# The last output tile computed as two column halves in PSUM tiles of their own, with a new order list

## The chip, the cores and the metric

The kernel runs on one core of a Trainium2 chip. The metric is the device time of one execution in microseconds (us), the median of several runs. TensorE is called PE below and its weight loads PEld, VectorE is DVE, ScalarE is ACT, GpSimd is POOL, SyncE is SP.

## The reference

An attention over pooled keys and values is followed by a gated feed-forward block, in float32:

```python
B, H, S, D = q.shape                       # 8, 8, 576, 64
k_p = k.reshape(B, H, S // 8, 8, D).mean(axis=3)     # 72 pooled keys
v_p = v.reshape(B, H, S // 8, 8, D).mean(axis=3)
attn = softmax(q @ k_p^T / sqrt(D))
x = (attn @ v_p) as (B, S, 512)
h = relu(x @ w_in)                         # w_in 512 x 1024
conv = sum over 3 taps of conv_w[k] * (h shifted along S)
out = (h * sigmoid(conv)) @ w_out          # w_out 1024 x 512
```

## The kernel before

The batch of 8 is worked through in order. The attention of a batch element makes pooled and transposed keys (`attn_k`), transposed queries (`attn_q`), scores with the exponential on ACT (`attn_s`), and the weighted values, normalised on DVE (`attn_av`, line 687 writes `xx`). `mm1` (line 747) computes the hidden layer in 8 blocks of 128 features, with relu on ACT (line 753). `conv` makes the gate in one of two ways: on ACT and DVE (`conv_off`), or by diagonal matrices on PE (`conv_pe`, line 800, its gate on ACT at line 805); line 838 multiplies gate and hidden layer into `gT`.

`mm2` (line 860) is the output product. Two batch elements make a pair of 1152 rows, which are 9 tiles of 128 rows and 512 columns. Each tile sums over 8 contraction blocks: 8 matmuls of 512 columns into one PSUM tile `psfB` or `psfA`, a copy to SBUF (`oe`, line 883) and a store from SP (line 887). In the last pair the tiles 4 to 8 are cut: blocks 0 to 5 first, blocks 6 and 7 when the last gate product has come. The last tile of all, tile 8, has `final` set. Its blocks 0 to 5 are six matmuls of 512 columns; blocks 6 and 7 are done twice, for the columns 0 to 255 and then 256 to 511, as four matmuls of 256 columns. All ten write the same PSUM tile. Two copies of 256 columns (line 873) on ACT and two stores (line 878) from SP follow, one for each half.

PSUM has eight slots: three pairs of banks, A0 to A2, and two single banks, B0 and B1. Nothing picks a slot at run time. `PARAMS["order"]` is a list, written out by a planner, of all 1075 operations in the order in which they are given to their engines. An entry `562@A1` says operation 562 with its output in slot A1; an entry `25A0/82@B1` says that 25 units of 128 columns of filler matmuls on zeros (`fill`, line 231; four units make one matmul of 512 columns) go to PE into slot A0 ahead of operation 82. An operation that takes a slot waits until the reader of that slot's former content is done. `PARAMS["act"]` says which of the copies and elementwise operations run on ACT; the others run on DVE.

The operations named later, by their numbers in the list:

- 77 `kT.0` and 79 `kz.0.1` (line 507): the first transposed keys and the second of their copies on ACT.
- 82, 80, 84 `qT.0...` (line 567): the first batch element's query transposes in three groups, 24, 24 and 48 small matmuls on PE, each with a copy on ACT (line 573). The first two need the first part of the load of `q` (line 250, 64 rows), the third needs the second part.
- 110 `sc.0.4.0` (line 627) and 111: the first scores on PE and their exponential on ACT (line 633).
- 266 `mm2.0.0.0`: the first output tile of the first pair.
- 562 `av.4.2` and 564 `nm.4.2`: weighted values of batch element 4 and their normalisation on DVE (line 687). 604 `mm1.3.5`, 464 `convs.2.1` (line 800) and 465, its gate on ACT (line 805).
- 661 and the DVE and ACT copies after it: the load of `q` for batch element 6 from POOL (line 255) and its regrouping (line 261).
- 1058 and 1062: the copies of tiles 5 and 6 of the last pair. 1068 to 1074: the last tile, in the order of the diff below.

Of the kernel before, what the change touches and what calls it, by code (L numbers as in the profile page):

```python
# [13 lines left out]

PARAMS = {
    "order": (
# [40 lines left out]
    ),  # L57
    "act": (
# [84 lines left out]
def kernel(  # L143
# [10 lines left out]
    nc = tc.nc  # L154
# [3 lines left out]
    P = 128  # L158
    HC = S // 2
    n_dc = d_model // P  # L160
    n_fb = d_ff // P
# [53 lines left out]
    pl = Planner()  # L215
# [17 lines left out]
    def copy_on(e):  # L233
        return nc.scalar.copy if e == "ACT" else nc.vector.tensor_copy
# [609 lines left out]
    def mm2(pair, tiles, cuts=(0, n_fb), kind="o", final=False):  # L844
# [5 lines left out]
        for x, t in enumerate(tiles):  # L850
# [1 line left out]
            key = (kind, pair, t)  # L852
            ok = ("op", pair, t)
            for c0, c1 in zip(cuts, cuts[1:]):
                parts = [(0, 512)] if not final or c1 < n_fb else [(0, 256), (256, 512)]
                for y, (j0, j1) in enumerate(parts):
                    def fn(e, t=t, c0=c0, c1=c1, key=key, j0=j0, j1=j1):
                        a = slot(key)
                        for c in range(c0, c1):
                            nc.tensor.matmul(out=a[:, 0, j0:j1], lhsT=g[:, c, t * P:(t + 1) * P],  # L860
                                             rhs=w_out[:, c, j0:j1], start=(c == 0), stop=(c == n_fb - 1), skip_group_check=final)
                    i = pl.add(f"mm2.{pair}.{t}.{c0}" + (f".{y}" if len(parts) > 1 else ""), "PE", (0.2165 * (j1 - j0) / 512 + 0.002) * (c1 - c0), fn,
                               reads=[("gT", pair % 2, c, z) for c in range(c0, c1) for z in halves] + [("wo", 0), ("wo", 1)]
                               + ([ok] if c0 else []),
                               writes=[ok + (y,)] if len(parts) > 1 else [ok], take=key,
                               after=last_o[0] if not c0 else None)
                    if not c0:
                        last_o[0] = i
            if final:
                oi = None  # L870
                for y in range(2):
                    def fn(e, y=y, key=key):
                        copy_on(e)(out=osb[i3][:, 0, y * 256:(y + 1) * 256], in_=slot(key)[:, 0, y * 256:(y + 1) * 256])
                    oi = pl.add(f"oe.{pair}.{t}.{y}", {"ACT": 0.28, "DVE": 0.34}, 0, fn,
                                reads=[ok + (y,)], writes=[("osb", i3, y)], give=key if y else None, after=oi)

                    def fn(e, y=y):
                        nc.sync.dma_start(out=out_rows[r:r + P, y * 256:(y + 1) * 256], in_=osb[i3][:, 0, y * 256:(y + 1) * 256])
# [89 lines left out]
```

## Time and profile before

| what | value |
|---|---|
| time, median of 3 runs | 198.35 us (197.63, 198.35, 200.87) |
| the profiled execution | 196.67 us |
| its span, first to last instruction | 195.0 us |
| mean granted TensorE clock | 1.000 |
| HBM read, written | 32.52 MB, 9.44 MB |
| matmuls on PE, weight loads | 1730, 1746 |

A row of the timeline has the start, the duration, engine, line, operation, names of output and inputs, shape and count, and in square brackets the idle time before it and what ended it. Instructions of one kind that follow each other are one row. A row of the chain of waits has the start, the duration and the work that the end of the execution can be followed back to. Instructions of one engine overlap: the duration of one is longer than the distance to the next. In a group's row stand count, busy time, mean duration in ns, and idle time before the group. Of the 1746 matmuls 16 have no record in this trace, their weight loads have.

### The profile page before, as it was taken

How to read it: one execution, taken by the hardware profiler on the slowest of the kernel's cores; microseconds unless marked ns; L12 is line 12 of the kernel's file. 1: busy time of each engine (PE TensorE's matmuls, PEld its weight loads, DVE VectorE, ACT ScalarE, POOL GpSimd, SP SyncE). 2: the span in 40 equal slices, each digit the busy share in tenths (PEclk: the TensorE clock that was granted, in tenths of full speed). 3: DMA queues.
4: the chain of work that ended last, by engine and by line, in shares of the span. 5: the costliest groups of instructions: out<-in, count | busy, mean ns of one | idle time of the engine just before them, and what ended most of it. 6: DMA issues, size and time to landing. Idle time of an engine off the chain costs nothing.

```text
span 195.0 us, 4515 instructions
## 1 busy us (share of the span) xinstructions
PE 186.5 (96%) x1730; PEld 124.3 (64%) x1746; DVE 166.1 (85%) x388; ACT 167.0 (86%) x301; POOL 46.7 (24%) x85
## 2 busy tenths in 40 slices
PE   7997999989999999999999999999999999999992
PEld 2465977665788878667667766685666566654441
DVE  3757789998589999999999899999999898999620
ACT  2088999955379999999999999999999999999931
POOL 8993354272055004363035000000000000000000
PEclk9999999999999999999999999999999999999999
DMA  5999999999939999999789999394003464105444
GB/s 193 210 163 202 203 203 208 203 206 204 152 50 172 203 205 157 195 96 201 152 135 180 200 296 140 89 186 118 14 0 95 151 196 170 54 0 217 170 156 161
DMA packets 40746, 30.72 MB, mean 158 GB/s; under 512 B 18556, under 2 KB 35668, under 8 KB 40724
## 3 DMA queue, kind: packets, MB, share of 16 engines
q0 software_dynamic: 17920, 15.67, 52.0%
q1 hardware_dynamic: 22804, 14.76, 30.2%
q8 instruction: 13, 0.21, 0.4%
q14 instruction: 9, 0.07, 0.1%
HBM read 32.52 MB, written 9.44 MB: 215 GB/s over the span
## 4 chain that ended last, share of the span: by engine, by line
PE 56%; ACT 17%; DVE 15%; DMA 8%; issue 2%; ACTq 0%; DVEq 0%
PE psfB L860 23%; PE psfA L747 17%; DMA q_b<-in_q_dram 5%; PE psfA L670 3%; ACT tg L788 3%; DMA osb<-in_k_dram 3%; ACT hT L753 3%; DVE gT L838 2%; DVE cv L776 2%; PE psfA L860 2%; DVE cv L781 2%; ACT cv L769 2%; DVE tg L832 2%; PE psfA L800 2%; PE psfA L674 2%
## 5 line engine op out<-in xcount | busy, mean ns | idle before, releaser
L860 PE MATMUL psfB<-w_out,gT 128*128 128x512 bf16 x260 | 62.2, 377 | 1.1 <-issue 0.3
L747 PE MATMUL psfA<-xT,w_in 128*128 128x288 bf16 x448 | 60.6, 286 | 0.0
L747 PEld LDWEIGHTS <-w_in 128*128 128x128 bf16 x448 | 43.3, 98 | 12.7 <-issue 0.2
L860 PEld LDWEIGHTS <-gT 128*128 128x128 bf16 x290 | 27.7, 98 | 30.4 <-issue 1.6
L788 ACT ACTIVATE tg<-cv,cs 128x576 bf16<-128x576 bf16 x54 | 42.2, 830 | 0.4 <-DVE cv L781 0.3
L753 ACT ACTIVATE hT<-psfA 128x576 bf16<-128x576 f32 x56 | 37.5, 692 | 4.8 <-PE psfA L747 4.5
L769 ACT ACTIVATE cv<-hT,cr 128x576 bf16<-128x576 bf16 x38 | 29.9, 830 | 0.0
L687 DVE TENSOR_TENSOR xx<-psfA,rr 128x512 bf16<-128x512 f32 x40 | 26.9, 687 | 0.7
L771 DVE TENSOR_SCALAR cv<-hT,cr 128x576 bf16<-128x576 bf16 x70 | 24.0, 369 | 1.1 <-ACT hT L738 0.7
L838 DVE TENSOR_TENSOR gT<-tg,hT 128x1152 bf16<-128x1152 bf16 x32 | 23.9, 754 | 0.4
L883 ACT COPY osb<-psfB 128x512 f32<-128x512 f32 x33 | 20.5, 643 | 4.2 <-PE psfB L860 3.0
L652 ACT ACTIVATE attnT<-psfA 128x576 bf16<-128x576 f32 x35 | 21.9, 664 | 0.5 <-PE psfA L644 0.3
L781 DVE TENSOR_TENSOR cv<-cv 128x1152 bf16<-128x1152 bf16 (+1 forms) x29 | 20.4, 710 | 1.1 <-ACT cv L769 0.5
L776 DVE TENSOR_TENSOR cv<-cv,hT 128x1152 bf16<-128x1152 bf16 (+1 forms) x29 | 20.5, 708 | 0.3 <-ACT cv L769 0.2
L295 POOL DMA_DIRECT2D v_b<-in_v_dram x32 | 16.3, 518 | 14.8 <-DVE vs L533 7.0
L670 PE MATMUL psfA<-vblk,attnT 128*128 128x130 bf16 x160 | 15.6, 221 | 1.3 <-ACT attnT L633 0.9
L832 DVE TENSOR_SCALAR tg<-tg 128x1152 bf16<-128x1152 bf16 x32 | 14.3, 454 | 1.6 <-ACT tg L788 1.5
L670 PEld LDWEIGHTS <-attnT 128*128 128x128 bf16 x160 | 11.8, 98 | 4.2 <-ACT attnT L633 1.3
L683 DVE RECIPROCAL rr<-psfA 128x8 f32<-128x8 f32 x40 | 7.3, 194 | 5.8 <-PE psfA L674 5.7
L231 PE MATMUL pswA<-zero 128*128 128x512 bf16 (+1 forms) x43 | 10.3, 385 | 1.1 <-DVE zero L333 1.1
L674 PE MATMUL psfA<-vblk,attnT 128*128 128x130 bf16 x80 | 11.2, 221 | 0.0
L644 PE MATMUL psfA<-qT,kz 128*128 128x288 bf16 x56 | 10.2, 286 | 0.1
(107 smaller groups left out, 220.4 us busy)
## 6 DMA issues: line engine op xcount, KB each, us to landing
out_dram<-osb SPq DMA_DIRECT2D x14, 512.0 KB, 3.7
q_b<-in_q_dram POOLq DMA_DIRECT2D x7, 576.0 KB, 9.4
k_b<-in_k_dram POOLq DMA_DIRECT2D x7, 512.0 KB, 10.0
v_b<-in_v_dram POOLq DMA_DIRECT2D x7, 512.0 KB, 8.4
out_dram<-osb SPq DMA_DIRECT2D x7, 256.0 KB, 2.2
osb<-in_k_dram SPq DMA_DIRECT2D x1, 1024.0 KB, 5.2
w_in<-in_moe_w_in_dram POOLq DMA_DIRECT2D x2, 512.0 KB, 10.1
w_out<-in_moe_w_out_dram POOLq DMA_DIRECT2D x2, 512.0 KB, 11.4
```

The source lines that it names most:

```text
L652: nc.scalar.activation(out=at(m)[:, t, :].rearrange("p (r i j) -> p r i j", i=2, j=3), in_=slot(key)[:, :, 0:HC].rearrange("p i (j r) -> p ...
L670: nc.tensor.matmul(out=a[:, g, c * w:(c + 2) * w], lhsT=attnT[m][:, S * s + u0:S * s + u0 + P], rhs=vblk[m][:, 2 * s:2 * s + 2, :].rearran ...
L687: nc.vector.tensor_tensor(out=xx[i3].rearrange("p (g h e) -> p g h e", g=2, h=4), in0=av_view()[:, :, :, 0:D], in1=rr[i3].rearrange("p (g ...
L747: nc.tensor.matmul(out=t[:, i, 0:HC], lhsT=w_in[:, c, f * P:(f + 1) * P], rhs=xT[m][:, c, i * HC:(i + 1) * HC], start=(c == 0), stop=(c == ...
L753: nc.scalar.activation(out=hT[m][:, f, 2:S + 2].rearrange("p (i x) -> p i x", i=2), in_=slot(key)[:, :, 0:HC], func=ACT.Relu)
L769: nc.scalar.activation(out=cv[y][:, kk // 2, z, :], in_=src, func=ACT.Copy, scale=sc)
L771: nc.vector.tensor_scalar(out=cv[y][:, kk // 2, z, :], in0=src, scalar1=sc, scalar2=None, op0=OP.mult)
L776: nc.vector.tensor_tensor(out=cv[y][:, 0, 0:n, :], in0=cv[y][:, 0, 0:n, :], in1=H4[:, f:f + n, 2:S + 2], op=OP.add)
L781: nc.vector.tensor_tensor(out=cv[y][:, 0, 0:n, :], in0=cv[y][:, 0, 0:n, :], in1=cv[y][:, 1, 0:n, :], op=OP.add)
L788: nc.scalar.activation(out=tg[i3][:, z, :], in_=cv[y][:, 0, z, :], func=ACT.Tanh if half else ACT.Sigmoid, scale=cs[:, f + z:f + z + 1] if ...
L838: nc.vector.tensor_tensor(out=o_, in0=tg[i3], in1=hT[b % 2][:, f:f + 2, 2:S + 2], op=OP.mult)
L860: nc.tensor.matmul(out=a[:, 0, j0:j1], lhsT=g[:, c, t * P:(t + 1) * P], rhs=w_out[:, c, j0:j1], start=(c == 0), stop=(c == n_fb - 1), skip ...
```

## The change

The last tile, number 8 of the last pair, takes two PSUM tiles, one for each half of its columns. Every contraction block is done in two matmuls of 256 columns, so that there are 16 matmuls of 256 columns in place of six of 512 and four of 256. By the new list the first half's eight come first, then the second half's eight. The first half is in slot B0, the second in B1. Each copy reads a PSUM tile of its own. The operation count rises by one, to 1076.

```diff
             for c0, c1 in zip(cuts, cuts[1:]):
-                parts = [(0, 512)] if not final or c1 < n_fb else [(0, 256), (256, 512)]
+                parts = [(0, 256), (256, 512)] if final else [(0, 512)]
                 for y, (j0, j1) in enumerate(parts):
+                    key = (kind, pair, t, y) if final else (kind, pair, t)
+                    ky = ok + (y,) if final else ok
+
                     def fn(e, t=t, c0=c0, c1=c1, key=key, j0=j0, j1=j1):
                         a = slot(key)
                         for c in range(c0, c1):
-                            nc.tensor.matmul(out=a[:, 0, j0:j1], lhsT=g[:, c, t * P:(t + 1) * P],
-                                             rhs=w_out[:, c, j0:j1], start=(c == 0), stop=(c == n_fb - 1), skip_group_check=final)
+                            nc.tensor.matmul(out=a[:, 0, 0:j1 - j0], lhsT=g[:, c, t * P:(t + 1) * P],
+                                             rhs=w_out[:, c, j0:j1], start=(c == 0), stop=(c == n_fb - 1))
...
             if final:
                 oi = None
                 for y in range(2):
+                    key = (kind, pair, t, y)
+
                     def fn(e, y=y, key=key):
-                        copy_on(e)(out=osb[i3][:, 0, y * 256:(y + 1) * 256], in_=slot(key)[:, 0, y * 256:(y + 1) * 256])
+                        copy_on(e)(out=osb[i3][:, 0, y * 256:(y + 1) * 256], in_=slot(key)[:, 0, 0:256])
                     oi = pl.add(f"oe.{pair}.{t}.{y}", {"ACT": 0.28, "DVE": 0.34}, 0, fn,
-                                reads=[ok + (y,)], writes=[("osb", i3, y)], give=key if y else None, after=oi)
+                                reads=[ok + (y,)], writes=[("osb", i3, y)], give=key, after=oi)
```

The order list is new as a whole. Sorted by engine, DVE, ACT, POOL and SP get exactly the operations that they had, in the order that they had. PE does too, but for the last tile and the fillers. What else is new in the list is the slots: 51 entries beside the last tile take another, where mostly two neighbours change places. Of the fillers some are moved and some are gone: 25 units ahead of the first query transposes (82) become 2, 2 ahead of the first scores (110) become 22, 10 at operation 305 become 3, and the single unit ahead of 266 is gone, as is the one ahead of 291; those ahead of 173, 178 and 183 change slot. The entries of which more is said:

```diff
-  ... 106A0/77@B0 ... 25A0/82@B1 ... 80@A0 ... 1A1/84@B0 ... 2A1/110@B1 106@A0 ...
+  ... 106A0/77@B0 ... 2A0/82@A0 ... 80@B1 ... 1A1/84@A1 ... 22A2/110@B0 63 106@B1 ...
-  ... 1B1/266@B1 ...
+  ... 266@B1 ...
-  ... 562@A1 560 557 604@A0 ... 464@A0 ...
+  ... 562@A0 604@A1 ... 464@A0 ...
-  1058 1055 1059 1061 1065 1062 1068@B0 1063 1066 1069 1070 1067 1071 1073 1072 1074
+  1058 1055 1059 1061 1065 1062 1068@B0 1063 1070 1069@B1 1066 1071 1067 1072 1074 1073 1075
```

In the last line 1068 before is blocks 0 to 5 of the last tile, 1069 and 1070 the two halves of blocks 6 and 7, 1071 and 1073 the copies, 1072 and 1074 the stores. After, 1068 and 1070 are the first half, 1069 and 1071 the second, 1072 and 1074 the copies, 1073 and 1075 the stores.

More of the change, by code (lines that the diff above doesn't have):

```diff
@@ L859, in fn @@
                         for c in range(c0, c1):
-                            nc.tensor.matmul(out=a[:, 0, j0:j1], lhsT=g[:, c, t * P:(t + 1) * P],
-                                             rhs=w_out[:, c, j0:j1], start=(c == 0), stop=(c == n_fb - 1), skip_group_check=final)
-                    i = pl.add(f"mm2.{pair}.{t}.{c0}" + (f".{y}" if len(parts) > 1 else ""), "PE", (0.2165 * (j1 - j0) / 512 + 0.002) * (c1 - c0), fn,
+                            nc.tensor.matmul(out=a[:, 0, 0:j1 - j0], lhsT=g[:, c, t * P:(t + 1) * P],
+                                             rhs=w_out[:, c, j0:j1], start=(c == 0), stop=(c == n_fb - 1))
+                    i = pl.add(f"mm2.{pair}.{t}.{c0}" + (f".{y}" if final else ""), "PE", (0.2165 * (j1 - j0) / 512 + 0.002) * (c1 - c0), fn,
                                reads=[("gT", pair % 2, c, z) for c in range(c0, c1) for z in halves] + [("wo", 0), ("wo", 1)]
-                               + ([ok] if c0 else []),
-                               writes=[ok + (y,)] if len(parts) > 1 else [ok], take=key,
+                               + ([ky] if c0 else []),
+                               writes=[ky], take=key,
                                after=last_o[0] if not c0 else None)
```

80 rows, old and new, of the table PARAMS are left out of this document.

## The prediction

> **What bounds the kernel now.** I read the page first, for the shares, and then the chain of waits, for what ends the execution.
>
> ```profile
> span 195.0 us, 4515 instructions
> ...
> PE 186.5 (96%) x1730; PEld 124.3 (64%) x1746; DVE 166.1 (85%) x388; ACT 167.0 (86%) x301; POOL 46.7 (24%) x85
> ...
> PE 56%; ACT 17%; DVE 15%; DMA 8%; issue 2%; ACTq 0%; DVEq 0%
> ```
>
> No engine bounds the whole: the chain changes from ACT and DVE to PE and back. So an edit counts only where the chain runs through it. The edit that the change is named for lies at the very end, so I go there next, to the last pieces of the chain and then to the timeline of the same stretch.
>
> ```profile
> 187.45 1.29 PE psfA L860 x6
> ...
> 189.61 1.75 PE psfB L860 x10
> 191.35 0.03 ACTq L873
> 191.38 0.04 issue
> 191.42 0.37 ACT osb L873
> ```
>
> ```profile
> 189.45 1.90 PE L860 MATMUL psfB<-w_out,gT 128*128 128x512 bf16 x10
> ```
>
> ```profile
> 190.74 0.60 PE L860 MATMUL psfB<-w_out,gT 128*128 128x256 bf16 x4
> ...
> 191.42 0.65 ACT L873 COPY osb<-psfB 128x256 f32<-128x256 f32 x2 [1.07 <-PE psfB L860]
> 191.82 0.81 SPq L878 DMA_DIRECT2D out_dram<-osb  x2
> ```
>
> All ten matmuls of the last tile are on the chain, and so is a copy after them. The first copy starts only when the whole tile is done: the four narrow matmuls end at 190.74 + 0.60 = 191.34, the copy starts at 191.42, and the first half's two of them were over about 0.22 earlier. ACT had then been idle for 1.07, and it was PE that it waited for. So the two copies and the two stores stand one behind the other at the end, and nothing covers them.
>
> **The change part by part: the last tile.** A narrow matmul lasts 0.273 by itself, and four of them 0.60.
>
> ```profile
> L860 PE MATMUL psfB<-w_out,gT 128*128 128x256 bf16 x4 | 0.6, 273 | 0.0
> ```
>
> One follows the other after (0.60 - 0.273) / 3 = 0.109. A wide one takes 1.29 / 6 = 0.215, so that the change, which makes 16 narrow ones of six wide and four narrow, adds 16 x 0.109 - 6 x 0.215 - 4 x 0.109 = 0.02 of PE. The weight loads rise from 10 to 16 at 0.098 each; I cost them at nothing, since they run beside the matmul before them. The block of line 747 shows that, where each matmul of 288 columns has its own load:
>
> ```profile
> L747 PE MATMUL psfA<-xT,w_in 128*128 128x288 bf16 x448 | 60.6, 286 | 0.0
> L747 PEld LDWEIGHTS <-w_in 128*128 128x128 bf16 x448 | 43.3, 98 | 12.7 <-issue 0.2
> ...
> L860 PEld LDWEIGHTS <-gT 128*128 128x128 bf16 x290 | 27.7, 98 | 30.4 <-issue 1.6
> ```
>
> ```profile
> 63.06 0.98 PE psfA L747 x8
> ```
>
> Eight with their loads take 0.98, or 0.1225 each for 288 columns, against 0.109 for 256: the ratio is that of the columns, with nothing left for 0.098. If that cover were gone, six more loads would cost 0.59.
>
> The Trainium skill's page "TensorE: Matmul & The Clock Gate" has a rule against this change, in "Part 3: Packing small matmuls — row/col tiling": a weight load overlaps a running matmul only where the two use different row groups, and here every one uses all rows. By it the six loads would be in the open, and the sum for the last tile would be a loss of 0.19 where the rows give a gain of 0.40. The trace disagrees (0.1225 a matmul with its load of 0.098), so I keep the rows and leave the rule a small chance.
>
> Now the order in time. The first half's eight start at 189.45, the eighth at 189.45 + 7 x 0.109 = 190.21, and it ends at 190.48. The first copy follows after the 0.08 of before, at 190.56, and lasts to 190.93. Two things could hold it. ACT must have done the copy of tile 7, and the store of tile 5 must have left the same SBUF buffer:
>
> ```profile
> 189.77 0.59 ACT L883 COPY osb<-psfA 128x512 f32<-128x512 f32 x1
> ```
>
> ```profile
> L887 SPq DMA_DIRECT2D out_dram<-osb x4: 332/338/345, 187.7 to 190.4; - x4
> ...
> DMA to landing us min/median/max: 2.0/2.1/2.2
> ```
>
> ACT is free at 190.36. Tile 5's store is the second of four and goes out after its copy's end, near 188.15; with 2.2 it is down near 190.35. Both come before 190.56. The second half's last matmul ends at 189.45 + 15 x 0.109 + 0.273 = 191.36, its copy starts at 191.44 in place of second in the row, and ends at 191.81; its store goes out at 191.84. Before, the second store went out at 191.82 + 0.81 - 0.38 = 192.25. From there on nothing differs: the landing takes 1.7, and the wind-down after it is the same.
>
> ```profile
> DMA to landing us min/median/max: 1.7/1.7/1.7
> ```
>
> Gain **0.40**. From below I bound it by the spacing of the two copies, 0.65 - 0.37 = 0.28, and from above by that of the two stores, 0.81 - 0.38 = 0.43.
>
> **The fillers at the start.** Here the list moves 23 units from ahead of the first query transposes to ahead of the first scores. What it moves them past is seen in PE's and ACT's timelines and in the loads of `q`.
>
> ```profile
> 9.48 1.54 PE L231 MATMUL pswA<-zero 128*128 128x512 bf16 x7
> 10.94 0.56 PE L567 MATMUL psbB<-ident,q_b 64*64 64x64 bf16 x24
> ...
> 11.98 0.93 PE L567 MATMUL psbB<-ident,q_b 32*64 32x32 bf16 x48
> 12.84 0.29 PE L231 MATMUL pswA<-zero 128*128 128x128 bf16 x2
> 13.10 0.35 PE L627 MATMUL psfB<-qT,kz 128*32 128x384 bf16 x4
> ```
>
> ```profile
> 10.70 0.39 ACT L507 COPY kz<-psbB 64x288 bf16<-64x288 bf16 x1
> 11.55 0.80 ACT L573 COPY qT<-psbB 128x768 bf16<-128x768 bf16 x1 [0.46 <-PE psbB L567]
> ...
> 13.65 0.50 ACT L633 ACTIVATE attnT<-psfB 128x384 bf16<-128x384 f32 x1
> ```
>
> ```profile
> L250 POOL DMA_DIRECT2D q_b<-in_q_dram x2: 602/722/841, 2.4 to 3.7; - x2
> ...
> DMA to landing us min/median/max: 7.1/7.3/7.5
> ```
>
> The two parts of `q` go out at 2.4 and 3.7 and are down by 2.4 + 7.5 = 9.9 and 3.7 + 7.1 = 10.8. The transposes of the first could go at 9.9, but start at 10.94, behind the fillers. Without these they start about 1.0 sooner, ACT is busy with the key copy until 11.09, and its query copies start there instead of at 11.55: 0.46 sooner at most. But then the fillers come back. The 48 transposes start near 10.95 and take 12.84 - 11.98 = 0.86, and 2816 columns of filler follow, at (10.94 - 9.48) / 3200 columns another 1.29. The scores start at 10.95 + 0.86 + 1.29 = 13.10: no sooner. Only their exponential gains: it needs the scores, done at 13.45, and no longer waits for ACT's third copy (until 13.65). I take **0.15**, between 0 and 0.46.
>
> **The filler ahead of 266.** The chain has it by name:
>
> ```profile
> 42.61 0.07 PE pswB L231
> 42.68 0.04 issue
> 42.72 2.75 PE psfB L860 x12
> ```
>
> It goes, and with it 0.07 + 0.04 = **0.11**; bounds 0 and 0.11. The other fillers that go stand on PE where the chain runs on ACT and DVE, and cost nothing now.
>
> **The slots.** A changed slot costs where its former reader ends after the taker could start. Going through the takers I find one that stands out. 464, a diagonal convolution on PE, follows 562 instead of 604 in slot A0, so it waits for 562's reader, the normalisation on DVE:
>
> ```profile
> 90.89 0.68 DVE L687 TENSOR_TENSOR xx<-psfA,rr 128x512 bf16<-128x512 f32 x1
> 90.92 0.10 PEld L800 LDWEIGHTS <-dw 128*128 128x128 bf16 x1
> ...
> 91.24 0.91 PE L800 MATMUL psfA<-hT,dw 128*128 128x288 bf16 x6
> ...
> 92.28 0.64 ACT L805 ACTIVATE tg<-psfA 128x576 bf16<-128x576 f32 x1
> ```
>
> DVE ends at 91.57; with 0.04 of hand-over PE starts at 91.61, not 91.24, and is done at 92.52. Queued behind it on PE is the next hidden block; behind its reader, the gate at line 805, is everything that ACT does. The gate starts at 92.56 instead of 92.28, and the chain runs through ACT there. Cost **0.28**; bounds 0, if ACT makes it up, and 0.65, from the weight load at 90.92 to the release at 91.57.
>
> **The sum.** -0.40 - 0.15 - 0.11 + 0.28 = -0.38. The profiled execution took 196.67 for its span of 195.0, and becomes 196.29. The median shown is 198.35, 1.68 above it, and becomes 197.97, or 198.0. By the bounds the sum lies between -0.43 - 0.46 - 0.11 = -1.00 and -0.28 + 0.65 = +0.37.
>
> **The rivals.** *All of the front's gain arrives and the slots cost nothing*: -0.40 - 0.46 - 0.11 = -0.97, 197.4. For it speaks ACT's idle 0.46 at 11.55, right on the chain; against it, that the scores start no sooner.
>
> *The slot wait decides, slower than before.* The load of `q` for element 6 stands between the front and the wait:
>
> ```profile
> 78.67 9.62 DMA q_b<-in_q_dram
> ...
> 88.39 1.47 ACT q L261
> ```
>
> If this landing does not move, whatever the front gains is gone by 88.39. After it come only the wait at 464 and the last tile. With the wait at its full 0.65 the sum is 0.65 - 0.40 = +0.25, 198.6. It decides from a wait of 0.40 on. Against it: the gate at line 805 starts only at 92.28 anyway, which leaves 0.28 of the wait.
>
> *The weight loads are in the open*: 0.59 - 0.40 = +0.19, 198.5. Line 747 speaks against it.
>
> *The last tile does not do what it says*: the first copy is still held to the end of all matmuls, and nothing else adds up: 198.35. For it, that a copy was held so before by matmuls whose columns it doesn't read; against it, the separate PSUM tiles.
>
> **How the numbers follow.** The forecast, 198.0, gets 0.46; the front's whole gain, 197.4, 0.22; the slot wait, 198.6, 0.22; weight loads in the open, 198.5, 0.04; no effect, 198.35, 0.06. The runs of before lie from 196.67 (profiled) to 200.87, so scatter is larger than any term. The low end is the profiled execution's own forecast, 196.3. The high end is the worst sum, 198.35 + 0.37 = 198.7, with a third of the way from the median to the highest run, 2.52 / 3 = 0.84: 199.6. Over 2%, which is about what a measurement of this kernel can tell from no change, would be 4 us. No case comes near, so 0.03 for each side is left to scatter, and 0.94 to within 2%.
>
> **What would show it.** Right: line 873's first copy starts about 0.9 ahead of the second and overlaps line 860; the second store goes out 0.5 after the last matmul's end, not 0.9; line 627 still starts near 13.1; line 800 starts late behind line 687 near 91.6. Wrong: the two copies of line 873 still back to back; 16 narrow matmuls taking over 1.9 (loads in the open); line 627 at 12.7 or earlier; a time under 196.3 or over 199.6, which would need a cause in the body that I have not found.

## The result, and the profile after

| | median, us | lowest to highest | runs | profiled execution, us | its span, us |
|---|---|---|---|---|---|
| before | 198.23 | 197.57 to 200.87 | 20 | 196.67 | 195.0 |
| the change | 197.36 | 195.85 to 200.32 | 20 | 196.76 | 195.1 |

The ratio of the change to the kernel before is 0.9941, with a 95% interval of 0.9921 to 0.9960. Ratios here and below leave out the executions that are over 1.5% above the fastest of their kernel, so they differ a little from the quotients of the medians. Of 198.23 that is a gain of 1.17 us, between 0.79 and 1.57. By the bound of 2% it is no difference; by its interval it is a gain, and about three times the forecast's 0.38. Yet the two profiled executions have the same span. So there are two questions: where the gain comes from, and where the profiled execution of the change lost it again.

The page of the changed kernel: the span, the busy shares, the clock row of the 40 slices and the shares of the chain.

```profile
span 195.1 us, 4522 instructions
...
PE 187.7 (96%) x1734; PEld 125.2 (64%) x1750; DVE 165.9 (85%) x388; ACT 167.3 (86%) x301; POOL 47.0 (24%) x85
...
PEclk9979999999999999999999999999999999999999
...
PE 80%; ACT 11%; DVE 6%; issue 2%; ACTq 0%
```

Each slice is 195.1 / 40 = 4.88 us. In the third, 9.8 to 14.6 us, the granted clock is 7 tenths; the kernel before showed no such slice. The chain is now 80% PE, where it was 56% before.

The end of the chain, and below it the timeline of the same stretch (start, duration, engine, line, operation, and in brackets the idle time ahead of it and what ended it). Lines 860, 873, 878 and 883 of before are 863, 878, 883 and 888 here.

```profile
190.22 1.76 PE psfB L863 x16
191.98 0.02 issue
192.00 0.37 ACT osb L878
```

```profile
190.05 1.91 PE L863 MATMUL psfB<-w_out,gT 128*128 128x256 bf16 x16
190.39 0.59 ACT L888 COPY osb<-psfA 128x512 f32<-128x512 f32 x1
191.17 0.37 ACT L878 COPY osb<-psfB 128x256 f32<-128x256 f32 x1 [0.19 <-PE psfB L863]
191.57 1.16 SPq L883 DMA_DIRECT2D out_dram<-osb  x2
192.00 0.37 ACT L878 COPY osb<-psfB 128x256 f32<-128x256 f32 x1 [0.46 <-PE psfB L863]
```

The first copy runs beside the second half's matmuls, 192.00 - 191.17 = 0.83 ahead of the second. Sixteen narrow matmuls, each with a weight load, take 1.76 on the chain, where ten took 1.75. The copy of tile 7 on line 888 ends at 190.98, which in the rows of before was 190.36 (0.59 from 189.77): the changed execution comes to the last tile 0.62 late. Its last copy ends at 192.37, before at 191.42 + 0.65 = 192.07, so only 0.30 late, and the second store goes out at 191.57 + 1.16 - 0.33 = 192.40 where it went at 192.25. The last tile has gained 0.62 - 0.15 = 0.47 up to that store.

So the profiled execution lost 0.6 ahead of the last tile. The table follows some operations: how much later each ended than in the trace of before. The runs beside the change are explained below.

| ended before at, us | operation | the change | e9, the change again | e10, slots back | e2, list alone | e4, fillers back | e11, fillers twice |
|---|---|---|---|---|---|---|---|
| 11.09 | key copy, line 507 | +0.09 | +0.72 | +0.21 | +0.38 | +0.21 | +0.11 |
| 16.56 | first values product | +1.02 | +0.46 | -0.04 | +0.07 | +0.26 | +1.06 |
| 42.48 | gate product, line 838 | +0.66 | +0.62 | +0.38 | -0.05 | +0.83 | +0.70 |
| 44.11 | 266, first output blocks | +0.38 | +0.34 | +0.11 | -0.33 | +0.56 | +0.43 |
| 68.48 | 532, query transposes | +0.51 | +0.47 | +0.11 | -0.20 | +0.69 | +0.56 |
| 93.53 | scores of element 5 | +0.90 | - | - | +0.19 | +1.08 | +0.95 |
| 102.71 | 790, scores of element 6 | +0.53 | - | - | -0.18 | +0.71 | +0.58 |
| 190.35 | copy of tile 7 | +0.63 | - | - | -0.10 | +0.76 | +0.65 |

(Where a dash stands, a load that landed late had shifted all that follows by over 2 us; it has a paragraph of its own below.) The key copy waits for a load, so its row is the run's own luck, and the next row is to be read against it. From 42.48 on the columns move in the same steps: -0.28 at 266, +0.13 at 532, about +0.4 by 93.53, then down by about 0.37, of which the last 0.26 is at 790. Ahead of that the change and e11 stand out, with over 1 us at the first values product. e11 has more fillers, as its paragraph says; the change has not.

The start of the changed execution, PE's timeline and one row of the windows view (busy time of PE, PEld, DVE, ACT and POOL, granted clock, DMA share, GB/s):

```profile
12.22 2.13 PE L231 MATMUL pswA<-zero 128*128 128x512 bf16 x6 [0.21 <-issue]
...
14.28 0.51 PE L627 MATMUL psfB<-qT,kz 128*32 128x384 bf16 x4
```

```profile
11.70:12.10 0.40, 0.31 (x19) 0.33 (x15) 0.18 (x1) 0.40 (x2) 0.40 (x2) 1.00 1.03 152
12.12:15.51 3.39, 3.29 (x14) 1.31 (x14) 2.57 (x8) 1.96 (x4) 3.21 (x5) 0.50 1.06 141
15.53:16.00 0.47, 0.47 (x5) 0.26 (x3) 0.00 (x0) 0.47 (x2) 0.00 (x0) 1.00 1.20 175
```

For some 3.4 us the clock was at half. The fillers ahead of the scores ran in it, and line 627 started at 14.28 instead of 13.10.

### The profile page after: what moved, and what is told of

Read it like the earlier page. It is cut to its first block, busy times and chain, and to the rows that moved or that the text cites. A ratio compares the mean times of both kernels' runs of the same rounds, so it can differ in the third digit from the quotient of the medians.

```text
span 195.1 us, 4522 instructions
## 1 busy us (share of the span) xinstructions
PE 187.7 (96%) x1734; PEld 125.2 (64%) x1750; DVE 165.9 (85%) x388; ACT 167.3 (86%) x301; POOL 47.0 (24%) x85
## 4 chain that ended last, share of the span: by engine, by line
PE 80%; ACT 11%; DVE 6%; issue 2%; ACTq 0%
PE psfB L863 26%; PE psfA L747 23%; PE pswA L231 6%; PE psfA L670 4%; PE psfA L800 3%; ACT tg L788 3%; PE psfA L644 2%; ACT cv L769 2%; PE psfA L732 2%; PE psfB L732 2%; ACT hT L753 2%; PE psbB L587 2%; PE psfA L674 2%; PE psfA L863 2%; PE psbB L701 2%
## 5 line engine op out<-in xcount | busy, mean ns | idle before, releaser
L863 PE MATMUL psfB<-w_out,gT 128*128 128x512 bf16 (+1 forms) x266 | 62.2, 372 | 1.0 <-issue 0.3
L863 PEld LDWEIGHTS <-gT 128*128 128x128 bf16 x296 | 28.3, 98 | 29.6 <-issue 1.4
L231 PE MATMUL pswA<-zero 128*128 128x512 bf16 (+1 forms) x41 | 11.2, 430 | 1.3 <-DVE zero L333 1.1
L507 ACT COPY kz<-psbB 64x288 bf16<-64x288 bf16 x12 | 4.7, 392 | 7.0 <-PE psbB L501 6.8
```

The costliest lines, as they stand in the source:

```text
L231: nc.tensor.matmul(out=t[:, 0:w * P], lhsT=zero[:, 0:P], rhs=zero[:, 0:1].to_broadcast([P, w * P]), start=True, stop=True)
L863: nc.tensor.matmul(out=a[:, 0, 0:j1 - j0], lhsT=g[:, c, t * P:(t + 1) * P], rhs=w_out[:, c, j0:j1], start=(c == 0), stop=(c == n_fb - 1))
```

## The experiments

All were timed in five rounds beside the kernel before. A ratio is a kernel's time over that of before, with its 95% interval.

| run | what it is | median, us | before, us | ratio |
|---|---|---|---|---|
| e1 | last tile alone | 197.79 | 198.10 | 0.9982 [0.9946, 1.0019] |
| e2 | list alone | 197.48 | 198.10 | 0.9964 [0.9928, 0.9999] |
| e3 | slots of 562 and 604 back | 196.95 | 198.10 | 0.9929 [0.9893, 0.9964] |
| e4 | fillers back | 197.59 | 198.10 | 0.9969 [0.9932, 1.0006] |
| e5 | before without the filler at 266 | 198.04 | 198.27 | 0.9996 [0.9957, 1.0035] |
| e6 | slots of 532, 562, 604 back | 197.19 | 198.27 | 0.9937 [0.9896, 0.9978] |
| e7 | slot of 790 back | 196.72 | 198.27 | 0.9957 [0.9916, 0.9997] |
| e8 | no fillers ahead of the first scores | 197.37 | 198.27 | 0.9993 [0.9957, 1.0029] |
| e9 | the change again | 196.90 | 198.34 | 0.9930 [0.9905, 0.9955] |
| e10 | e6 again | 196.45 | 198.34 | 0.9924 [0.9884, 0.9965] |
| e11 | fillers at both places | 197.95 | 198.34 | 0.9982 [0.9952, 1.0012] |

An interval is some 0.5 to 0.8 us wide to each side, so single terms of 0.1 to 0.3 can't be read from times. They are read from the traces. The mean granted clock is on record for every execution, not for the profiled ones alone; it is counted behind e11.

**e1: the last tile alone.** The list of before up to 1062, then the change's last line and its code.

```diff
-  ... 1062 1068@B0 1063 1066 1069 1070 1067 1071 1073 1072 1074
+  ... 1062 1068@B0 1063 1070 1069@B1 1066 1071 1067 1072 1074 1073 1075
```

> The list of before up to the last tile, and the last tile as in the change. Theory (the last tile saves what its rows said, about 0.40 to 0.53 us, and the rest of the change's gain of about 1.2 us comes from the new list): 0.4 to 0.55 us under before, a ratio near 0.9975; first copy of line 878 about 0.83 ahead of the second and overlapping line 863; everything ahead of the last tile as before. Rival (the whole gain is the last tile's): a ratio near 0.994. Rival (the last tile gains nothing because the landings end the execution anyway): 1.000.

The end of its chain and its two stores:

```profile
190.66 1.76 PE psfB L863 x16
192.43 0.02 issue
192.45 0.37 ACT osb L878
```

```profile
192.02 1.16 SPq L883 DMA_DIRECT2D out_dram<-osb  x2
```

The same shape as in the change: sixteen in 1.76, and the second store at 192.02 + 1.16 - 0.33 = 192.85. Its copy of tile 7 was 1.07 late against before, the store 192.85 - 192.25 = 0.60, so the last tile gains 0.47 here too. The time shows 0.36, in an interval that holds both 0 and 1.07. The delay ahead of the last tile was not expected, since this kernel has before's list: it too had a stretch of half clock, later than the change's.

```profile
16.14:19.53 3.39, 3.01 (x29) 2.69 (x30) 1.82 (x5) 1.98 (x8) 0.51 (x1) 0.50 1.22 198
```

**e2: the list alone.** The change's list up to 1062 with before's last tile: the code of before, and

```diff
-  ... 1062 1068@B0 1063 1070 1069@B1 1066 1071 1067 1072 1074 1073 1075
+  ... 1062 1068@B0 1063 1066 1069 1070 1067 1071 1073 1072 1074
```

> The new list up to the last tile, and the last tile as it was before. Theory: it keeps what the list brings, 0.5 to 0.8 us under before, a ratio of 0.996 to 0.9975, with runs in which the clock dips near the start and others in which it doesn't. Rival (the gain is all the last tile's): 1.000. Rival (the slot wait decides): 1.001 or more.

The ratio gives 0.71; with e1's 0.36 that makes 1.07, near the change's 1.17. So the list brings a part of the gain of its own. Which part is the larger the times don't show: e1's interval reaches from a loss of 0.38 to a gain of 1.07, e2's from 0.02 to 1.43. The trace had full clock throughout and no part of its last tile overlaps: the two copies are one row, as before.

```profile
191.31 0.65 ACT L873 COPY osb<-psfB 128x256 f32<-128x256 f32 x2 [1.06 <-PE psfB L860]
```

**e3: the slot wait at 464 undone.**

```diff
-  774 522 562@A0 604@A1 ...
+  774 522 562@A1 604@A0 ...
```

> The change, but 562 and 604 have the slots of before, so that 464 no longer waits for the normalisation of 562. Theory (that wait costs 0.36 us on the chain, as the trace after shows between ACT's +0.46 and +0.82): 0.3 us faster than the change, a ratio to before of about 0.9925; line 800 near 92 starts when its turn comes. Rival (a later wait takes it back, since PE and ACT wait for each other again near 102): the same as the change, 0.994.

In the changed kernel the wait is there as forecast, in DVE's, PE's and ACT's rows:

```profile
91.40 0.68 DVE L687 TENSOR_TENSOR xx<-psfA,rr 128x512 bf16<-128x512 f32 x1
...
92.13 0.92 PE L800 MATMUL psfA<-hT,dw 128*128 128x288 bf16 x6 [0.19 <-DVE xx L687]
...
93.09 0.65 ACT L805 ACTIVATE tg<-psfA 128x576 bf16<-128x576 f32 x1 [0.24 <-PE psfA L800]
```

DVE ends at 92.08, PE starts at 92.13 and names it. DVE's row is 0.51 later than before (90.89), PE's 0.89 (91.24), the gate 0.81 (92.28): the wait costs 0.38 on PE and 0.30 at the gate. With the two slots back PE no longer follows DVE:

```profile
92.39 0.68 DVE L687 TENSOR_TENSOR xx<-psfA,rr 128x512 bf16<-128x512 f32 x1
...
92.54 0.91 PE L800 MATMUL psfA<-hT,dw 128*128 128x288 bf16 x6
```

PE starts 0.53 ahead of DVE's end. The mechanism is shown. The time, 196.95, lies between the change's two medians, 197.36 and 196.90 (e9), and tells nothing of 0.3.

**e4: the fillers back where they were, all else as in the change.**

```diff
-  2A0/82@A0 ... 22A2/110@B0
+  25A0/82@A0 ... 2A2/110@B0
```

> The change, but the 23 filler units stand ahead of the query transposes again, with the new slots. Theory (the move gains at most 0.15 us in an execution with the full clock, and in some executions the clock drops to half near 12 us, which costs over 1 us there): as fast as the change or up to 0.3 us faster, ratio 0.992 to 0.9945, with the spread of its runs narrower; clock 1.00 throughout, line 627 near 13.1. Rival (the move of the fillers is where the list's gain comes from): 0.4 to 0.5 us slower than the change, 0.9965.

PE's rows with the fillers ahead of the transposes (e4), then ahead of the scores (e10, which has the change's fillers), both at full clock:

```profile
9.70 1.54 PE L231 MATMUL pswA<-zero 128*128 128x512 bf16 x7
...
13.53 0.35 PE L627 MATMUL psfB<-qT,kz 128*32 128x384 bf16 x4
```

```profile
12.11 1.38 PE L231 MATMUL pswA<-zero 128*128 128x512 bf16 x7
13.42 0.35 PE L627 MATMUL psfB<-qT,kz 128*32 128x384 bf16 x4
```

The key copy was 0.21 late in both, so by it the scores start 0.43 - 0.21 = 0.22 later than before in e4, and 0.11 later in e10: no sooner, as forecast. By the first values product e4 is 0.05 behind before and e10 0.25 ahead (e9 0.26, e2 0.31). So the new places of the fillers are worth 0.30 with the new slots, and the new list as a whole 0.25 to 0.31 there, if the clock stays full. The time went the rival's way: 0.9969, where the theory had 0.992 to 0.9945 and the rival 0.9965, in an interval that holds all of these. Nor was the clock full throughout: in 6 of its 12 executions it was not.

**e5: the kernel before, without the one filler ahead of 266.**

```diff
-  1B1/266@B1
+  266@B1
```

> The kernel before, and of all the change only the one filler unit ahead of 266 gone. Theory (that one unit costs 0.28 us on the chain, the step between 40 and 45 us in every trace with the new list): in the trace line 838's last product before it and the first matmul of line 860 come 0.28 closer, and all later work keeps it; time 0.28 us under before, 0.9986, too little for the times to tell. Rival (prediction's 0.11): 0.11 closer. Rival (what was gained there came from the slots near it): nothing.

Its trace makes the same step as the change's: +0.53 at the gate product, +0.25 at 266, a gain of 0.28. The chain's row had priced the filler at 0.11. The timelines of before and of the change at this place show why:

```profile
42.45 0.22 PE L231 MATMUL pswB<-zero 128*128 128x128 bf16 x1
...
42.72 0.38 PE L860 MATMUL psfB<-w_out,gT 128*128 128x512 bf16 x1
```

```profile
42.88 0.39 PE L701 MATMUL psbB<-ident,xx 128*128 128x128 bf16 x4
...
43.10 0.38 PE L863 MATMUL psfB<-w_out,gT 128*128 128x512 bf16 x1
```

Four transposes take 0.39, a single one 0.22, so that they start (0.39 - 0.22) / 3 = 0.057 apart. The last starts at 43.05, and the output matmul follows 0.05 behind. Before, the filler followed the last transpose in the same way, but the output matmul came 42.72 - 42.45 = 0.27 after the filler: it writes the slot that the filler wrote, and starts only 0.05 after the filler's end at 42.67. So the filler costs its whole duration with its hand-over, not the 0.06 at which PE could issue past it. The Trainium skill's page "TensorE: Matmul & The Clock Gate", "Part 2: What happens when you issue a matmul", has a formula for a single matmul at full clock, by which 128 columns take an estimated (398 + 128) / 2.4 = 219 ns, much more than its gap in a stream; the row's 0.22 agrees. The time shows nothing (0.9996): the gain is smaller than the interval, and later in e5's trace the load of `q` for element 6 takes it back, ACT being 0.26 late at 87 and 0.05 early at 190.35 in spite of the key copy's 0.13.

**e6 and e10: the slots of 532, 562 and 604 back**, with that of 345 and those of the four operations near 117 us. e10 is the same kernel once more.

```diff
-  532@A0 345@A1 ... 562@A0 604@A1 ... 685@A0 ... 711@A2 ... 689@A0 ... 739@A2
+  532@A1 345@A0 ... 562@A1 604@A0 ... 685@A2 ... 711@A0 ... 689@A2 ... 739@A0
```

> The change, with the slots of before for the takers that the traces show later by their new ones: 532 and 345, 562 and 604, 685, 711, 689 and 739. Theory (these cost 0.13 near 68 us, 0.36 near 92 and 0.05 near 117, and nothing takes it back): 0.54 us faster than the change, a ratio to before of about 0.9915, the fastest of all. Rival (a later wait takes it back): as the change, 0.994.

> The changed kernel with the list of before's slots for the operations 532, 562 and 604 (and their neighbours), for a profiled execution in which no late load lies. Theory: without the wait near 68 us (0.13) and the one near 92 us (0.36) the span is 0.3 to 0.5 shorter than the changed kernel's at equal clock, near 194.2; what is lost on the slots shows at no later place. Time 196.9 (196.3 to 197.5). Rival: the landing of a load near 88 us sets the pace there whatever the slots are, and the span and the time are those of the change, 197.4.

The chain of before and of the change at 532, a set of query transposes on PE:

```profile
68.28 0.34 PE psbA L587 x16
```

```profile
68.66 0.47 PE psbA L587 x16
```

The second set of sixteen takes 0.13 longer in the change. With the slots back the step is gone: +0.11 at 44.11 and +0.11 at 68.48 in e10. Both profiled executions then met the late load, so their spans (197.6 and 197.1) do not answer what was expected of them. Their ratios are 0.9937 and 0.9924, the change's 0.9941 and 0.9930. e6's is the rival's number, not the theory's 0.9915; e10's 196.45 lies in the range expected of it. That this version beats the change is not shown.

**e7: the slot of 790 back.**

```diff
-  790@A2 618 602@A0
+  790@A0 618 602@A2
```

> The change, with the slots of before for 790 and 602, the scores near 102 us. Theory (the new slot lets these scores start 0.26 us sooner, on the chain, a gain that the prediction overlooked): 0.26 slower than the change from 103 us on, ratio 0.9955; the lag that 464 causes near 92 stays to the end. Rival (PE and ACT make the lag of 464 up in any case): the lag goes down near 104 all the same, ratio 0.994.

The change at 790, its scores on line 644 between hidden blocks of line 747, and e7:

```profile
102.78 0.53 PE L747 MATMUL psfA<-xT,w_in 128*128 128x288 bf16 x3
103.14 0.41 PE L644 MATMUL psfA<-qT,kz 128*128 128x288 bf16 x2
103.43 0.28 PE L747 MATMUL psfA<-xT,w_in 128*128 128x288 bf16 x1
```

```profile
107.75 0.65 PE L747 MATMUL psfA<-xT,w_in 128*128 128x288 bf16 x4
108.52 0.41 PE L644 MATMUL psfA<-qT,kz 128*128 128x288 bf16 x2
108.76 0.65 PE L747 MATMUL psfA<-xT,w_in 128*128 128x288 bf16 x4
```

And the kernel before:

```profile
99.73 2.74 PE L747 MATMUL psfA<-xT,w_in 128*128 128x288 bf16 x21
102.61 0.40 PE L644 MATMUL psfA<-qT,kz 128*128 128x288 bf16 x2
```

In the change the scores start 0.17 ahead of the modelled end of the block before them (102.78 + 0.53 = 103.31), as matmuls in a stream do. In e7 they start 0.12 after that end (108.40), before 0.14 after it (102.47): there they wait for their slot. So the change gains 0.26 at 790, and e7 gives it back. The time can't tell it: 196.72, but a ratio of 0.9957.

**e8: no fillers ahead of the first scores either.**

```diff
-  22A2/110@B0
+  2A2/110@B0
```

> The change, with 2 filler units ahead of the first scores in place of 22. Theory (the fillers hold the scores back, and are there for the clock): scores at 12.6 in place of 13.1, their exponential 0.2 to 0.4 us sooner, and in executions with the full clock 0.2 to 0.4 us faster; but a drop of the clock near 12 us in more of the executions, with 1.2 us lost at the start, so that the median is between 0.3 faster and 0.3 slower than the change. Rival (the fillers have no part in the clock): always 0.2 to 0.4 us faster, 0.992 to 0.993.

```profile
12.06:18.87 6.81, 5.75 (x44) 3.78 (x42) 4.55 (x13) 5.52 (x15) 4.02 (x7) 0.50 1.06 149
```

The scores start at 12.70, sooner than anywhere else, but the clock is at half from 12.06 to 18.87, twice as long. By 25.60 the trace is 0.69 behind before, with a key copy only 0.04 late. The ratio, 0.9993, is the highest of all runs with the new last tile, but the median, 197.37, is that of the change, as the theory had it; the interval is too wide to say more. What is clear is the clock: in all 12 executions its mean was 0.991 or less, so all had such a stretch. The rival, that the fillers have no part in the clock, falls.

**e9: the change again.** Nothing is edited.

> The changed kernel once more, for a second profiled execution. Theory (the half clock at the start is a matter of chance, not of the new list): if this execution has the full clock throughout, the scores of line 627 start within 0.2 us of 13.10 after the landing of the key load is allowed for, not 1.2 later, and the span is 194.4 to 194.8 instead of 195.1; the second half copy again ends 0.3 sooner than the work before it would have it. Rival (moving the fillers takes the clock away every time): the clock is at half again from about 12 to 15.5 us. The time should lie within 0.4 per cent of 197.4 in either case.

The clock was full to 90 us. The scores were 0.82 late with a key copy 0.72 late: 0.10, not 1.2. So the new list does not bring the half clock every time. The span that was expected can't be read, because of a load that landed late (below). Of the profiled executions with the change's fillers, two had it near the start (the change and e3) and five had not (e2, e6, e7, e9, e10); of those with the old fillers e1 had it, and before, e4 and e5 had not.

**e11: fillers at both places.**

```diff
-  2A0/82@A0
+  25A0/82@A0
```

> The changed kernel with fillers at both places: 25 units ahead of the query transposes, as before, and 22 ahead of the first scores, as after. Theory: the 23 more units of filler cost what the path through the scores has no cover for, so that the first scores start 0.9 to 1.3 later than in the kernel before (14.0 to 14.4) at full clock, and 0.3 to 0.6 of that is left at 45 us; the time is 197.6 to 198.0. Rival (fillers pay by holding the clock, which would else drop in most executions): the time is under 197.2, and no half clock shows.

```profile
13.21 1.38 PE L231 MATMUL pswA<-zero 128*128 128x512 bf16 x7
14.52 0.35 PE L627 MATMUL psfB<-qT,kz 128*32 128x384 bf16 x4
```

Scores 1.42 late, just over the expected 1.3, and +0.43 left at 44.11. Of the rival, that fillers pay by holding the clock, one half came: no half clock shows, and none of the 12 executions has a mean clock under 0.994. The other half did not: 197.95 is not under 197.2. In the traces of the change and of e11 a stretch of half clock and 23 units of filler too many cost alike, some 1.0 at the values product and 0.4 at 44 us.

**How often the clock drops.** One stretch of 3.4 us at half clock takes 1.7 / 195 = 0.009 off the mean clock of an execution. So a mean of 0.992 or less tells that the clock has dropped, though not where.

| kernel | executions | clock dropped | median of the others, us | median of these, us |
|---|---|---|---|---|
| before, timed beside e1 to e11 | 90 | 58 | 197.22 | 198.48 |
| the change (with e9) | 26 | 8 | 196.93 | 198.30 |
| e4, fillers back | 12 | 6 | 196.82 | 198.57 |
| e8, no fillers ahead of the first scores | 12 | 12 | - | 197.37 |
| e11, fillers at both places | 12 | 0 | 197.95 | - |

All executions are counted here. The kernels with the fillers ahead of the transposes (before, e1, e4, e5) have a drop in 77 of 126, those with the fillers ahead of the scores (the change, e2, e3, e6, e7, e9, e10) in 22 of 83. e8 and e11 differ from the change by fillers alone, so the fillers near the start bear on how often the clock drops: with 2 units at each of the two places it dropped every time, with 25 and 22 never. e4 by itself, 6 of 12, is too little to tell the two places apart. In e6, e7 and e9 the drop that the profile shows came after a late load, not near the start; of the executions without a profile only the count is known.

This is the larger part of the gain. The mean of all executions goes from 198.10 for before to 197.42 for the change, by 0.68. The executions of before with a drop have a mean of 198.61, those without one 197.18. So the smaller share of drops is worth (58/90 - 8/26) x (198.61 - 197.18) = 0.48, and 0.20 is left for everything else. Shares so far apart would come by chance in 3 of 1000 cases (Fisher's exact test). Between executions without a drop the medians are 0.29 apart, with an interval (95%, by resampling) from a loss of 0.30 to a gain of 0.61. The clocks of before are from the rounds of the experiments, since those of the rounds of the result are not on record; in e9's own rounds the drops are 15 of 20 and 2 of 6.

**The late load.** In the profiled executions of e6, e7, e9 and e10 a transposing load of line 710 that goes out near 83 us landed late. The chain of e9 and of e10:

```profile
83.97 7.95 DMA xT<-xx
91.91 0.04 issue
91.95 3.49 PE psfA L747 x15
```

```profile
83.61 8.67 DMA xT<-xx
92.27 0.04 issue
92.31 2.00 PE psfA L747 x15
```

Ahead of the hidden block PE had nothing to do, and in e9 (as in e6 and e7) the clock then dropped to half, so that fifteen matmuls took 3.49 instead of 2.00. In e10 it stayed full. Of the profiles with before's list (before, e1, e5) none has such a load; whether the new list makes it likelier is not shown. These traces are read only up to 90 us, and at 790 by the step alone.

## Why the prediction was right or wrong

The time lies in the range and within 2% of before. The forecast's gain of 0.38 was too small: the interval begins at 0.79. The rival of the front's whole gain gave 197.4, the number that came out, but not for its reason, as the points show.

**The step that failed most: from the profile to the median.** The prediction works out what the profiled execution gains, and carries its distance to the median, 1.68, over unchanged. But the profiled execution of before had a granted clock of 1.000, and 58 of 90 executions of before had a drop: their median is 198.48, that of the others 197.22. So most of that distance is the 1.26 between these two, and it is not a constant: the change has a drop in 8 of 26. The prediction treated the fillers as work that delays the scores, and put their part in the clock at nothing without a reason. By the means this part was 0.48 of 0.68, more than the whole forecast of 0.38. That the time still fell into the range is owed to its width.

**The last tile: right.** 0.47 by the traces of the change and of e1, against 0.40, just over the upper bound of 0.43. The order was as worked out: first copy 0.83 ahead (0.9 forecast), second store at 192.40, or 0.44 after the modelled end of the last matmul at 190.05 + 1.91 = 191.96 (0.5 forecast). Of the 0.07 above the forecast, 0.04 is the hand-over from the last matmul to its copy: 192.00 - 191.96 = 0.04, where 0.08 was taken from before.

**The weight loads in the open: wrong, as argued.** Sixteen with their loads in 1.76 leave nothing for six times 0.098. The rule of the Trainium skill's page "TensorE: Matmul & The Clock Gate", "Part 3: Packing small matmuls — row/col tiling", taken as the prediction takes it, does not hold for these matmuls. The same section also lets a load go ahead that targets a background weight buffer; that the loads run beside the matmuls agrees with it, but no trace shows the buffer.

**The fillers at the start: the mechanism right, the size low, and one thing not foreseen.** The scores start no sooner, as worked out; the list gains 0.25 to 0.31 at the values product where 0.15 was taken, inside the bounds. What the prediction did not have is the clock, as said above.

**The filler ahead of 266: the term that was mis-sized most among those named.** 0.28 against 0.11, above its upper bound. What failed here is to price an instruction on PE by its pieces on the chain. They show what the filler added beyond the pipelined end of its forerunner; what it costs is the wait of the next matmul for the filler's own end.

**The slots: 464 right, the search wrong.** 464 costs 0.30 at the gate, 0.28 forecast. But "going through the takers I find one that stands out" failed: there are more. 532 costs 0.13, 693 some 0.05 near 117 us, and 790 gains 0.26; e6, e10 and e7 show that these steps go when the slots go back. A former reader that now ends earlier than before was not looked for. 206, a hidden block that ended at 25.60 before, gains 0.17: the delay falls from 1.02 to 0.86 there in the change, and from 0.46 to 0.29 in e9. No run puts its slot back.

**The sum by the traces:** -0.47 for the last tile, -0.25 at the start, -0.28 at 266, and 0.63 - 0.38 = +0.25 for all slots from 44 us on: -0.75. With the 0.17 of 206 it is -0.92, where no load comes in between. This is a sum for an execution at full clock, against the one profiled execution of before. That it agrees with the measured 0.79 to 1.57 is in part luck, since the measured gain is mostly the clock; where the clock did not drop the times show 0.29, and at most 0.61. How much of the single waits is lost again to the loads stays open: the row of the key copy alone differs by up to 0.7 from one execution to the next, and no run here was fine enough.

## What to carry to other kernels

Look at the granted clock of all executions before explaining a median: here the larger part of the gain is that the clock drops in fewer of them, and the fillers near the start bear on that. A new order changes many single waits of 0.1 to 0.4 besides: go through every slot for a reader that ends sooner as well as for one that ends later. Price a filler by its full duration where the next matmul writes the same PSUM slot, not by its spacing in a stream. And one profile may hold a stretch of half clock or a late load that another execution of the same kernel doesn't have: compare step by step along the trace, and take a second profile before blaming the change.

## What the hardware showed that was not expected

Stretches of half clock come in one length, 3.4 us, or twice that (e8, and e7 after its late load), and start at another time in each execution: near 12.1 in the change and in e8, 12.6 in e3, 16.1 in e1, between 91.0 and 92.3 in e6, e7 and e9. The clock rows of before, e2, e4, e5, e10 and e11 show none. The Trainium skill's page "TensorE: Matmul & The Clock Gate", "Part 1: The HAM clock gate (the "warmup" mystery)", tells of an activity window of 3413 ns that runs freely, whatever the kernel's start; the lengths and the changing starts agree with it.

How long PE is idle does not decide it alone: PE waited 1.9 for the late load in e9, and the clock dropped; it waited 2.8 in e10, and the clock stayed full. The traces show a pattern, which no run was made to test. Divide a trace into steps of 3.413 us from its first clock record, and count the columns of the matmuls in each, every matmul weighted by the share of the array's rows and columns that it uses. A step full of fillers holds 8192. The step ahead of each of the seven stretches holds 1988 to 2832. Of the other steps at full clock, up to the last matmuls, one holds 2640 (e2), all the rest 2960 or more. In e10 the idle time falls into two steps, with 3244 and 5760, in e9 into one, with 2572. Fillers fill such steps, and where the steps lie changes from one execution to the next.

The transposing load of line 710 took about 8 us or more to land in four profiled executions. In before its six issues between 76 and 96 us took

```profile
DMA to landing us min/median/max: 2.4/3.8/6.3
```

What holds it at times was not tried.
